# A planned attention and MLP kernel: w_in and w_out gated on block 1's values, the second buffer set's constant rows gated on w_out, and new planner constants

## The chip, the core and the metric

The kernel runs on one core of a Trainium2 chip. The time is the device time of one execution in microseconds (us). The core has five engines with their own instruction streams, which meet through semaphores: PE (TensorE, matrix products), ACT (ScalarE), DVE (VectorE), POOL (GpSimd) and SP (SyncE, which here only starts transfers). Transfers started by SP, ACT and POOL run on 16 DMA engines.

## The reference

Inputs are q, k, v of shape (4, 8, 768, 64), w_in (512, 2048) and w_out (2048, 512), all float32.

```python
ub = np.sum(np.maximum(q[:, :, :, None, :] * k_min[:, :, None, :, :],
                       q[:, :, :, None, :] * k_max[:, :, None, :, :]), axis=-1)
ub = np.where(causal, ub, -1000000000.0)
top_chunks = np.argsort(ub, axis=-1)[..., -top_k:]      # top 6 of 24 chunks of 32 keys
scores = scale * np.matmul(q, k.transpose(0, 1, 3, 2))
mask = sel & (pos[:, None] >= pos[None, :])
attn = softmax(np.where(mask, scores, -1000000000.0))   # written out in the reference
x = (attn @ v), heads put side by side                  # 3072 x 512
h = x @ w_in
g = np.maximum(h, 0.0) + np.log1p(np.exp(-np.abs(h)))
out = g @ w_out
```

So each query attends to the six chunks of keys with the highest upper bound, and the result goes through a two-layer MLP with a softplus.

## The kernel before, in words

**Blocks.** The queries are cut into 12 blocks of 256 rows: 4 batches of 3 blocks each. Block n belongs to batch n // 3. Each block has a preparation (`prep`), four attention units, one for each pair of heads (`attend`), and an MLP (`mlp_h`, `mlp_y`). The keys, values and chunk bounds of a batch live in one of two buffer sets, chosen by batch number modulo 2; block 3 is the first that uses the second set.

**Preparation.** k and q are transposed (blocks 0 to 2, the ramp, by PE at L515 and L572; later blocks by DMA at L534 and L582). DVE takes the maxima and minima of each chunk (L522, L538). ACT copies k into `ka` and `kb` (L519) and q into `qb` (L576); DVE makes the positive and negative parts of q (L591). PE computes the upper bounds (L611, L612), DVE masks them, finds the sixth largest and marks the chunks below it (L618 to L638). These marks are transposed (L659 or L674) and stand as extra rows in q; the matching extra rows of `ka` and `kb` hold a one-hot pattern of the chunks, so that the score matmul itself subtracts a large number for chunks not chosen.

**Attention.** For each head, L714 makes scores in PSUM, L723 takes the exponential on ACT, L729 cuts the diagonal on POOL, L740 multiplies by v, whose column of ones yields the sum; L749 and L761 normalize on DVE, and the result is transposed into x (L769, L774 in the ramp; by DMA at L777 later).

**MLP.** L797 multiplies x by w_in, L803 and L807 make the softplus on ACT as ln(1 + exp), L823 multiplies by w_out, L828 copies the result out of PSUM, L833 stores it.

**The planner.** The program is first built as a graph of tasks, each with an engine, a duration, a priority (a due time, lower first) and dependencies. `schedule` simulates the engines with these numbers: an engine that is free takes the ready task of lowest priority number for which buffers are free. The order found is then emitted, and each engine executes its part strictly in that order; what the hardware does later or earlier than planned doesn't change it. Before plan time `WARM` (30 us), whenever PE has nothing ready, the planner puts a filler in its stream, a matmul on a tile of zeros (L366).

Transfers have their own model: one started at plan time t enters its engine's queue `DMA_START` later; the queues share the DMA engines in proportion to a packet cost (`pkt`: 18 for block loads, 172 for a w_in half, 98 for a quarter of w_out); a transfer counts as landed `lat` after its last packet. At most 8 transfers of SP and ACT are under way.

**Loads.** Block loads of the ramp (`ramp_loads`, L398 and L401) come in two halves of 256 KB for each of q, k, v; they are issued in the order of `ORDER`. w_in comes in two transfers (i01, i23; L445), w_out in four (o0 to o3; L448), all issued by POOL, which converts them to bf16 on the way. Two kinds of holds tie these streams: `hold_pool` is a tiny POOL copy that reads a block's landed tile (L457), so that the weight loads behind it on POOL can't be issued earlier; `HOLDS` names the tile. `hold_sp` is a tiny SP transfer that reads a landed weight (L463), so that the loads behind it on SP can't be issued earlier. Before the change the first hold of POOL reads the second half of q of block 1 and stands ahead of w_in; SP's hold on the first w_in transfer stands ahead of k, q, v of block 2; POOL's second hold reads the second half of q of block 2 and stands ahead of w_out; SP's last hold (`LGATE`), on the third w_out transfer, stands ahead of the loads of block 3 and later blocks (L426).

**Due times.** `when_att` and `when_mlp` give each attention unit and MLP unit a due time. `MSTART` is where the MLP's due times start; `AOFF` and `AEND` say after how much MLP work the attention of blocks 3 to 11 begins and before how much of it that attention ends. `RLEAD` is how much earlier than its attention the preparation of blocks 0, 1, 2 is due, `POST` how much later the normalizing work of these blocks, `OPRIO` the priority of w_out's issue, `LEAD` how much earlier than the attention the loads of a later block are due.

**The second set's constants.** `background(1, ...)` (L349 to L355) clears `bd`, writes the column of ones of v, clears rows 0 to 31 of `kb` on DVE, and copies the one-hot rows into `ka` and `kb` by two POOL transfers.

Of the kernel before, what the change touches and what calls it, by code (L numbers as in the profile page):

```python
# [13 lines left out]
ACT = mybir.ActivationFunctionType  # L14
# [22 lines left out]
COLD = 4.2  # L37
TD = 1.9
TLAT = 1.4
RLEAD = (1, 1, -1)  # L40
POST = (0, 5, -2)
OPRIO = 15
LEAD = 18
BG = 40
DMA_START = 1.3
MSTART = 16
AOFF = 16
PADD = 0.0
PLEAD = 12
AEND = 26  # L50
ORDER = "k0 q0 k1 v0 q1 v1 i01 i23 k2 q2 v2 o0 o1 o2 o3".split()
HOLDS = [("q", 1, 1), ("q", 2, 1), ("q", 2, 1)]
SHIFT = (0, 0, 8)


# [21 lines left out]
class Graph:  # L77
# [7 lines left out]
    def add(self, eng, dur, fn, prio, r=(), w=(), dma=None, lat=None, name="", after=(), pkt=18, port=None, alt=None, at=0.0):  # L85
        t = Task()
        t.n, t.eng, t.dur, t.fn, t.prio, t.dma, t.name = len(self.tasks), eng, dur, fn, prio, dma, name
        t.lat = LAT[eng] if lat is None else lat
        t.pkt = pkt
        t.port = port if port is not None else eng == "POOL" and dma is None  # L90
        t.alts = {eng: (dur, fn, t.port)}
        if alt:
            t.alts[alt[0]] = (alt[1], alt[2], False)
        deps, bufs = set(after), []
        for key in list(r) + list(w):
            b = key[0] if isinstance(key, tuple) else key
            if isinstance(b, Buf) and b not in bufs:
                bufs.append(b)
        for key in r:
            if key in self.last:  # L100
                deps.add(self.last[key])
            self.readers.setdefault(key, []).append(t)
        for key in w:
            if key in self.last:
                deps.add(self.last[key])
            deps.update(x for x in self.readers.pop(key, ()) if x is not t)
            self.last[key] = t
        t.deps, t.users, t.bufs = deps, [], bufs
        for d in deps:
            d.users.append(t)  # L110
        for b in bufs:
            b.left += 1
        t.wait, t.ready, t.start, t.end, t.order = len(deps), at, None, None, None
        self.tasks.append(t)
        return t

    def schedule(self):
# [8 lines left out]
        def post(at, what, x):  # L126
            nonlocal seq
            seq += 1
            heapq.heappush(events, (at, seq, what, x))
# [59 lines left out]
        while True:  # L189
            nxt = events[0][0] if events else None  # L190
            live = [q for q in queues.values() if q]
            if live:
                total = sum(q[0][2] + (1 if len(live) > 1 else 0) for q in live)
                cand = moved + min(q[0][0] * total / q[0][2] for q in live)
                if nxt is None or cand < nxt:
                    nxt = cand
            if nxt is None:
                break
            now = max(now, nxt)
            flow(now)  # L200
            while events and events[0][0] <= now + 1e-9:
                _, _, what, x = heapq.heappop(events)
                if what == "ready":
                    for a in x.alts:
                        heapq.heappush(ready[a], (x.prio, x.n, x))
                elif what == "free":
                    free[x.pool].append(x.slot)
                    if x.kind:
                        used[x.pool, x.kind] -= 1
                elif what == "unlock":  # L210
                    x[0].held[x[1]] -= 1
                elif what == "landed":
                    x.end = now
                    done(x, now)
                elif what == "queue":
                    queues.setdefault(x.eng, []).append([x.dma, x, x.pkt])
            for e in LAT:
                if idle[e] > now + 1e-9 or not ready[e] and (e != "PE" or spare is None):
                    continue
                held, got = [], None  # L220
                while ready[e]:
                    item = heapq.heappop(ready[e])
                    if item[2].start is not None:
                        continue
                    if fits(item[2], e):
                        got = item[2]
                        break
                    held.append(item)
                for item in held:
                    heapq.heappush(ready[e], item)  # L230
                if e == "PE" and spare is not None and now >= WARM:
                    free["ps"].append(spare)
                    spare = None
                if got is None and e == "PE" and spare is not None and self.filler is not None \
                        and self.filler.deps and all(d.end is not None and d.end <= now for d in self.filler.deps):
                    self.fills.append((len(order), spare))
                    order.append(self.filler)
                    idle[e] = now + self.filler.dur * (2 if now < COLD else 1)
                    post(idle[e], "tick", None)
                if got is None:  # L240
                    continue
                t = got
                t.eng = e
                t.dur, t.fn, t.port = t.alts[e]
                if len(t.alts) > 1:
                    t.lat = LAT[e]
                for b in t.bufs:
                    if b.pool == "ps":
                        b.held[t.eng] = b.held.get(t.eng, 0) + 1
                    if b.slot is None:  # L250
                        b.slot = free[b.pool].pop(0)
                        if b.kind:
                            used[b.pool, b.kind] = used.get((b.pool, b.kind), 0) + 1
                t.start = now
                if t.port:
                    port[t.eng] = now + t.dur
                order.append(t)
                if e == "PE" and now < COLD:
                    t.dur *= 2
                idle[e] = now + t.dur  # L260
                post(idle[e], "tick", None)
                if t.dma is None:
                    t.end = now + t.dur + t.lat
                    done(t, t.end)
                else:
                    if e != "POOL":
                        flying.append(t)
                    post(now + DMA_START, "queue", t)
        assert len(order) == len(self.tasks) + len(self.fills), (len(order), len(self.tasks))
        return order  # L270

# [1 line left out]
def build(nc, tiles):  # L273
# [75 lines left out]
    def background(i, pr, after, blks):  # L349
        add("DVE", 0.2, lambda: DV.memset(T("bd", i), 0.0), pr, w=[("bd", i)], name="bd0", after=after)  # L350
        add("DVE", 0.1, lambda: DV.memset(T("v", i)[:, :, :, D:D + 1], 1.0), pr, w=[("v1", i)], name="v1", after=after)
        add("DVE", 1.35, lambda: DV.memset(T("kb", i)[0:32], 0.0), pr + 2, w=[("kb0", i)], name="kb0", after=after)
        for which in ("ka", "kb"):
            add("POOL", 0.6, lambda which=which: PO.dma_start(*oh(which, i, blks)), pr, r=["ohb"],
                w=[(which + "c", i, k_) for k_ in blks], name="oh" + which, after=after, dma=0.8, pkt=200, lat=0.7)  # L355
# [34 lines left out]
    def ramp_loads(nm, n, base, gate):  # L390
        for t in range(2):
            b_ = XF[nm, n, t] = Buf("xf")
            pr = base + 0.1 * t
            if n == 0 and nm != "v":
                for u, eng in ((0, "SP"), (1, "ACT")):
                    def ld(nm=nm, t=t, b_=b_, u=u, q_=AC if u else SP):
                        dst = T(b_).rearrange("s (t h d) -> s t h d", t=NT, d=D)
                        q_.dma_start(out=dst[:, u], in_=rows(nm, n, u)[:, t * 4:t * 4 + 4])  # L398
                    add(eng, 0.6, ld, pr, w=[(b_, u)], dma=0.585, lat=0.5, name=f"ld{nm}{n}{t}", after=gate)
            else:  # L400
                add("SP", 0.6, lambda nm=nm, t=t, b_=b_: SP.dma_start(  # L401
                    out=T(b_).rearrange("s (h d) -> s h d", d=D), in_=rows(nm, n, t)), pr,
                    w=[(b_, 0), (b_, 1)], dma=1.17, lat=0.5, name=f"ld{nm}{n}{t}", after=gate)


    def columns(nm, n, hh, p, t):
# [432 lines left out]
    for n in range(NRAMP):  # L839
        for p in range(NP):  # L840
            attend(n, p)
    background(1, BG, [landed["w_in", 3]], [0, 1, 2])
    for n in range(NB):
        m = n + NRAMP
        mlp_h(n)
# [114 lines left out]
```

## Time and profile before

| | |
|---|---|
| median of 7 runs | 261.6 us |
| lowest, highest | 260.17, 263.49 us |
| profiled execution, its own time | 260.04 us |
| span of its profile | 258.3 us |
| PE busy | 250.8 us (97%) |
| ACT busy | 202.9 us (79%) |
| DVE busy | 150.3 us (58%) |
| POOL busy | 84.5 us (33%) |
| HBM read, written | 27.26 MB, 6.29 MB |
| granted clock of PE | 0.999 of full |

The page of a profile gives busy times of the engines, the span in 40 slices (each digit the busy share in tenths), groups of instructions by line with their count and mean duration, and the transfers. The timeline lists instructions in order: start, length, engine, line, operation, written tile <- read tiles, form, count; an engine's idle time before an instruction and what ended it stand in brackets. PE's matmuls are pipelined: the length of one is longer than its distance to the next, so PE counts as busy where its starts are close. POOLq, SPq and so on stand for the issuing of a transfer, not for its running.

### The profile page before, as it was taken

The page shows a single profiled execution, that of the slowest core. Times are in us where ns is not written, and L with a number is a line of the kernel's source. Part 1 is how long each engine was busy: PE and PEld are TensorE (multiplying, and loading weights), DVE is VectorE, ACT ScalarE, POOL GpSimd, SP SyncE. Part 2 cuts the span into 40 slices and gives each one's busy share as a digit, 9 for nine tenths or more (in the row PEclk, how much of TensorE's full clock was granted, in tenths as well). Part 3 has the DMA queues.
Part 4 walks back from the last instruction along what each step waited for, and adds up shares of the span by engine and source line. Part 5 has one row for each costly group of instructions (what it writes and reads, how often), then busy time and mean ns, then how long its engine had stood idle before and what let it go on. Part 6 is the DMA issues. An engine that isn't in the chain of part 4 may idle for free.

```text
span 258.3 us, 6762 instructions
## 1 busy us (share of the span) xinstructions
PE 250.8 (97%) x2563; PEld 191.5 (74%) x2594; DVE 150.3 (58%) x549; ACT 202.9 (79%) x369; POOL 84.5 (33%) x179
## 2 busy tenths in 40 slices
PE   8999999999999999999999999999999999999994
PEld 6989996687685885788677678777677777776763
DVE  7797565347796699546998586665964211211101
ACT  5795999999296995899679779968689799666470
POOL 5180470255235470354805425235022111100000
PEclk9999999999999999999999999999999999999999
DMA  7989999999996996998679899649511220230202
GB/s 174 255 144 213 251 183 188 219 239 228 185 260 129 235 219 137 271 193 189 145 181 241 170 224 197 154 123 206 121 44 41 43 82 3 23 102 0 82 2 82
DMA packets 119993, 39.90 MB, mean 154 GB/s; under 512 B 113528, under 2 KB 115832, under 8 KB 119960
## 3 DMA queue, kind: packets, MB, share of 16 engines
q1 hardware_dynamic: 114456, 34.09, 60.5%
q0 software_dynamic: 3392, 4.85, 10.5%
q10 hardware_dynamic: 2112, 0.52, 0.9%
q8 instruction: 20, 0.33, 0.5%
q14 instruction: 13, 0.11, 0.1%
HBM read 27.26 MB, written 6.29 MB: 130 GB/s over the span
## 4 chain that ended last, share of the span: by engine, by line
PE 80%; DMA 10%; DVE 3%; SPq 2%; POOL 2%; issue 2%; ACT 0%; DVEq 0%
PE ps L823 28%; PE ps L797 28%; PE ps L714 12%; PE ps L740 7%; DMA w_out_sb<-in_moe_w_out_dram 5%; DMA w_in_sb<-in_moe_w_in_dram 3%; PE ps L366 3%; DMA w<-in_q_dram 2%; SPq L401 2%; POOL w_out_sb L448 1%; PE ps L515 1%; PE ps L612 1%; POOL pt L729 1%; DVE kx L538 1%; PE ps L611 1%
## 5 line engine op out<-in xcount | busy, mean ns | idle before, releaser
L797 PE MATMUL ps<-x,w_in_sb 128*128 128x256 bf16 x768 | 101.6, 272 | 0.2
L723 ACT ACTIVATE pt<-ps 128x512 bf16<-128x512 f32 (+1 forms) x192 | 94.2, 609 | 8.6 <-PE ps L714 8.3
L823 PE MATMUL ps<-w_out_sb,g 128*128 128x512 bf16 (+1 forms) x369 | 92.0, 370 | 1.5 <-DMA w_out_sb<-in_moe_w_out_dram 0.2
L797 PEld LDWEIGHTS <-w_in_sb 128*128 128x128 bf16 x768 | 72.4, 98 | 15.1
L729 POOL TENSOR_SCALAR_AFFINE_SELECT pt<-pt 128x256 bf16<-128x256 bf16 x96 | 40.2, 425 | 123.4 <-ACT pt L723 123.3
L803 ACT ACTIVATE e<-ps 128x512 f32<-128x512 f32 x96 | 59.8, 646 | 26.5 <-PE ps L797 26.2
L823 PEld LDWEIGHTS <-g 128*128 128x128 bf16 x400 | 36.7, 98 | 25.7 <-ACT g L807 0.6
L807 ACT ACTIVATE g<-e 128x1024 bf16<-128x1024 f32 x48 | 52.6, 1095 | 1.0
L828 DVE COPY yo<-ps 128x512 f32<-128x512 f32 (+1 forms) x25 | 16.7, 669 | 41.1 <-PE ps L823 40.9
L749 DVE RECIPROCAL st<-ps 128x4 f32<-128x4 f32 x48 | 8.5, 179 | 43.5 <-PE ps L740 38.3
L714 PE MATMUL ps<-qab,kb 128*128 128x256 bf16 x192 | 30.6, 259 | 0.1
L740 PEld LDWEIGHTS <-pt 128*128 128x128 bf16 x672 | 26.4, 97 | 4.2
L714 PE MATMUL ps<-qab,ka 96*128 96x256 bf16 x192 | 29.1, 259 | 0.1
L740 PE MATMUL ps<-v,pt 128*128 128x65 bf16 x672 | 28.1, 193 | 0.1
L436 POOL CAST w<-w 128x512 bf16<-128x512 f32 x36 | 22.5, 637 | 2.2 <-DMA w<-in_k_dram 1.8
L538 DVE TENSOR_REDUCE kx<-w 128x32 bf16<-128x1024 bf16 x18 | 21.2, 1208 | 0.1
L714 PEld LDWEIGHTS <-ka 96*128 96x128 bf16 x192 | 17.5, 98 | 5.1 <-issue 0.2
L714 PEld LDWEIGHTS <-kb 128*128 128x128 bf16 x192 | 16.6, 97 | 5.3
L366 PE MATMUL ps<-zero 128*128 128x256 bf16 x118 | 17.2, 290 | 1.1 <-DVE zero L336 1.1
L761 DVE TENSOR_TENSOR w<-ps,st 128x256 bf16<-128x256 f32 x36 | 15.1, 422 | 1.2
L627 DVE MAX8 ub<-ub 128x8 f32<-128x24 f32 (+2 forms) x160 | 14.5, 163 | 0.3
L366 PEld LDWEIGHTS <-zero 128*128 128x128 bf16 x118 | 11.5, 104 | 2.9 <-DVE zero L336 1.1
(64 smaller groups left out, 179.5 us busy)
## 6 DMA issues: line engine op xcount, KB each, us to landing
w<-in_v_dram SPq DMA_DIRECT2D x24, 256.0 KB, 4.4
out_dram<-yo SPq DMA_DIRECT2D x23, 256.0 KB, 2.2
w<-in_k_dram SPq DMA_DIRECT2D x22, 256.0 KB, 3.8
w<-in_q_dram SPq DMA_DIRECT2D x22, 256.0 KB, 4.2
w_in_sb<-in_moe_w_in_dram POOLq DMA_DIRECT2D x2, 1024.0 KB, 10.5
w_out_sb<-in_moe_w_out_dram POOLq DMA_DIRECT2D x4, 512.0 KB, 8.6
w<-in_k_dram SPq DMA_DIRECT2D x2, 128.0 KB, 3.0
w<-in_k_dram ACTq DMA_DIRECT2D x2, 128.0 KB, 3.6
```

The costliest lines, as they stand in the source:

```text
L366: PE.matmul(T(Fill)[:, 0:256], T("zero")[:, 0:128], T("zero"), start=True, stop=True)
L436: PO.tensor_copy(T(b_)[:, :, t], T(xf).rearrange("s (p c) -> s p c", p=NP))
L538: DV.tensor_reduce(T(kx)[:, m].rearrange("d p (t c) -> d p t c", t=NT), T(kt).rearrange("d (p t) (c s) -> d p t c s", t=NT, s=CH), axis=AX ...
L714: PE.matmul(T(sp)[:, z * QB:z * QB + QB - q0], kk[r0:r1, p, (j + z) * 128:(j + z + 1) * 128], qq[r0:r1, p, q0:QB], start=True, stop=True)
L723: AC.activation(T(pt)[:, j:j + 2].rearrange("k j c -> k (j c)")[:, 0:w], T(sp)[:, 0:w], ACT.Exp, scale=SCALE)
L729: PO.affine_select(out=diag, in_=diag, compare_op=ALU.is_ge, fill=0.0, base=0, channel_multiplier=-1, pattern=[[0, 2], [1, 128]])
L740: PE.matmul(o[:, u, h], T(pts[h])[:, j, c0:c0 + 128], T("v", i)[:, j, 2 * p + h, :], start=(j == 0), stop=(j == t0 + u))
L797: PE.matmul(o, T("w_in")[:, dt, ft * 128:(ft + 1) * 128], T(x)[:, dt], start=(dt == 0), stop=(dt == KDM - 1))
L803: AC.activation(T(e)[:, f2 * 2:f2 * 2 + 2].rearrange("f a s -> f (a s)"), T(hp), ACT.Exp)
L807: AC.activation(T(gb)[:, f4 * 4:(f4 + 1) * 4], T(e), ACT.Ln, bias=1.0)
L823: PE.matmul(T(y)[:, 0:w], T(gb)[:, f, u * 128:(u + 1) * 128], T("w_out")[:, f, cs], start=(f == 0), stop=(f == KFF - 1))
L828: add("DVE", 0.06 + 0.54 / parts, lambda y=y, yo=yo, w=w: DV.tensor_copy(T(yo)[:, 0:w], T(y)[:, 0:w]), pr, r=[y], w=[yo], name=f"yo{n}")
```

## The change

Ten planner constants get other values; `DMA_START` becomes a table, with 2.5 us for POOL's transfers instead of 1.3; the planned landing latency of the ramp's block loads goes from 0.5 to 0.7 us. `ORDER` puts k, q, v of block 2 ahead of the weights: with that, SP's hold between the first w_in transfer and block 2's loads no longer exists, POOL's second hold ahead of w_out no longer exists, and the one hold left, ahead of all six weight transfers, reads the first half of v of block 1. `LGATE` still reads the third w_out transfer. The second set's constants wait in the plan for the second w_out transfer instead of the second w_in transfer.

```diff
-RLEAD = (1, 1, -1)
-POST = (0, 5, -2)
-OPRIO = 15
-LEAD = 18
+RLEAD = (3, 6, 3)
+POST = (2, 0, 0)
+OPRIO = 20
+LEAD = 14
 BG = 40
-DMA_START = 1.3
-MSTART = 16
-AOFF = 16
+DMA_START = {"SP": 1.3, "ACT": 1.3, "POOL": 2.5}
+MSTART = 18
+AOFF = 8
 PADD = 0.0
 PLEAD = 12
-AEND = 26
-ORDER = "k0 q0 k1 v0 q1 v1 i01 i23 k2 q2 v2 o0 o1 o2 o3".split()
-HOLDS = [("q", 1, 1), ("q", 2, 1), ("q", 2, 1)]
+AEND = 20
+ORDER = "k0 q0 k1 v0 q1 v1 k2 q2 v2 i01 i23 o0 o1 o2 o3".split()
+HOLDS = [("v", 1, 0), ("k", 2, 1), ("k", 2, 1)]
...
-                    post(now + DMA_START, "queue", t)
+                    post(now + DMA_START[e], "queue", t)
...
-                    add(eng, 0.6, ld, pr, w=[(b_, u)], dma=0.585, lat=0.5, name=f"ld{nm}{n}{t}", after=gate)
+                    add(eng, 0.6, ld, pr, w=[(b_, u)], dma=0.585, lat=0.7, name=f"ld{nm}{n}{t}", after=gate)
...
-                    w=[(b_, 0), (b_, 1)], dma=1.17, lat=0.5, name=f"ld{nm}{n}{t}", after=gate)
+                    w=[(b_, 0), (b_, 1)], dma=1.17, lat=0.7, name=f"ld{nm}{n}{t}", after=gate)
...
-    background(1, BG, [landed["w_in", 3]], [0, 1, 2])
+    background(1, BG, [landed["w_out", 1]], [0, 1, 2])
```

## The prediction, made before the changed kernel was run

> **What bounds the kernel now.** I read the page's busy times first, then the slices, then the timeline of the first 50 us, the spacing of matmuls over the whole trace, and ACT's busy time by stretch.
>
> ```profile
> PE 250.8 (97%) x2563; PEld 191.5 (74%) x2594; DVE 150.3 (58%) x549; ACT 202.9 (79%) x369; POOL 84.5 (33%) x179
> ...
> PE   8999999999999999999999999999999999999994
> ...
> DMA  7989999999996996998679899649511220230202
> ...
> L366 PE MATMUL ps<-zero 128*128 128x256 bf16 x118 | 17.2, 290 | 1.1 <-DVE zero L336 1.1
> ```
>
> PE looks full everywhere, but line 366 is the planner's filler: 118 matmuls on zeros, all before 23.4 us, 14.4 us by their start-to-start spacing. Useful matmuls had used only 7.9 us when the first MLP matmul (L797) started at 24.34. After that the spacing shows almost no holes up to the last matmul start at 254.7: records missing from the trace leave about 31 apparent gaps of 0.22 us, and the larger ones are 0.72 us at 92.2, 0.48 at 67.1, 0.32 at 49.3. True waiting after 24.34 is about 1.5 us, and 3.6 us follow the last start. So the time is set by how much useful PE work is done by about 25 us, and by not opening holes later: 258.3 us = 14.4 filler + about 2 of early waiting + 1.5 + 3.6 + about 237 of work and its ordinary spacing.
>
> The start of the MLP hangs on the first w_in half:
>
> ```profile
> 15.52 0.18 POOL L457 CAST scratch<-w 1x1 bf16<-1x1 f32 x1
> 15.65 1.53 POOL L445 DMA_DIRECT2D w_in_sb<-in_moe_w_in_dram  x2
> 16.65 0.64 PE L572 MATMUL ps<-identf,w 128*128 128x128 f32 x4
> ...
> 23.51 0.55 PE L714 MATMUL ps<-qab,ka 96*128 96x256 bf16 x4
> ...
> 23.71 0.29 DVE L774 COPY x<-ps 128x256 bf16<-128x256 bf16 x1 [0.22 <-PE ps L769]
> ...
> 23.85 0.75 SPq L463 DMA_DIRECT2D scratch<-w_in_sb  x1
> ...
> 24.34 0.60 PE L797 MATMUL ps<-x,w_in_sb 128*128 128x256 bf16 x4
> ...
> 34.99 3.02 POOL L448 DMA_DIRECT2D w_out_sb<-in_moe_w_out_dram  x4
> ...
> 40.50 1.90 PE L823 MATMUL ps<-w_out_sb,g 128*128 128x512 bf16 x7
> ```
>
> The reader sees hold, w_in issue, w_in landed (SP's hold passes at 23.85), first MLP matmul; block 1's first scores (L714) and the end of block 0's last copy into x fall at the same moment. w_out follows only at 34.99 and its first use waits at 40.50. In the packets, the block loads stream without a break from 2.0 to 15.4 us (256 KB each 1.05 us), then nothing moves until 17.3; w_in takes 17.3 to 28.0, block 2's loads 28 to 35.5, another hole of 1.2 us, w_out 36.4 to 48.2.
>
> The second bound is ACT, by stretch:
>
> ```profile
> 20.00:24.34 4.34, 1.89 (x4) 1.00 1.12 212
> 24.34:35.00 10.66, 10.66 (x23) 1.00 1.18 250
> 35.00:40.00 5.00, 4.93 (x9) 1.00 0.84 139
> ```
>
> Second column: length of the stretch, then ACT's busy time. It idles 2.45 us just before the MLP starts and then has none to spare for 15 us.
>
> **The change, part by part.** Filler and order are fixed by the planner, so I work its constants by hand for positions only; durations are the trace's. Plan time plus 0.8 is trace time here: w_in's first landing is planned at 22.85, so 23.65, and SP passed at 23.85.
>
> 1. Gate of w_in. In the plan block loads take 1.17 each; the second part of q1 ends at 14.87, the first of v1 at 16.04, and landing is 0.5, now 0.7, later. The hold moves from 15.37 to 16.74; with start 2.5 for 1.3 and the k2 loads beside it (rate 172/192, so 4.9 becomes 5.47), w_in's first landing is planned at 25.57, 26.4 in trace time. The first MLP matmul goes from 24.34 to 26.4 to 27.0: **2.0 to 2.7 us later**, with filler or other work ahead of it. The data itself hardly moves: the old hold did not wait for q1 at all but for the four selects before it on POOL (14.00 to 15.57). One or two more selects (0.4 each, their exps done by 17) may now stand before it: issue 15.7 to 17.3, landing 8.2 later, 24 to 25.5, plus sharing with k2. So mostly the plan, not the data, is late.
>
> 2. What fills these 2 us. Block 1's prep gets priority 6 ahead of its time instead of 1, ahead of block 0's post (2 later). From qT (16.65) to its first scores (23.5) the chain took 6.8 us. In it, block 0's work stands on DVE: two reciprocals and two normalizations after 19 us (0.18 + 0.41 each, 1.2 in all) and one pair with an x copy before 18.1 (0.9); on ACT an exp and an x copy stand between the two qb copies (0.9, beside the DVE work). So scores start 1.2 to 2.1 earlier, 21.4 to 22.3. Four exps take 1.9 us (0.48 each): 8 to 10 of 16 by 26.4, with three more scores in flight 11 to 13 at 0.22 or 0.16, some 2.3; one or two pairs of value products (14 x 0.029 = 0.41 each); and the transposes of k2, landed by 18 because its loads now follow v1 directly (8 x 0.109 = 0.87). Useful PE work by 26.4 was 9.85 before; now 6.92 (all before the first scores) + 0.2 + 2.3 + 0.4 to 0.8 + 0.87 = 10.7 to 11.1, or 10.2 with late scores. Ahead by 0.4 to 1.2.
>
> 3. Keeping it. From 24.34 to 35 ACT was full, so PE's lead survives only as far as ACT too is ahead. It is, by what it uses of the 2.45 idle: 1.2 to 2.1, less k2's copies taken early. Steps 1 to 3: between 0 and 1.9, I take **-0.9**, the middle.
>
> 4. w_out. Its issue moves from 34.99 to about 20 (POOL is 0.76 per issue and free from 19.6 to 25). Queue 0 needs 10.7 + 11.5 = 22.2 us of packets; from about 18 that ends at 40.2, or 44 if all of block 2's 6 loads not yet moved (6.3 less 2.6 moved in today's hole) go first. Before it was 48.2. The first output matmul can leave 40.5 for about 35; the waits at 40.5 and 49.3 and their neighbours go, about 0.5. **-0.4**; not more, because PE had other matmuls to do while it waited.
>
> Who yields is not in the trace for this pair. Nearest rows: k2, issued at 25.04, got not one packet until 27.7 while w_in ran, which gives the block loads no share; the one-hot transfer at 30.25 to 31.0 left q2 a share of about 0.37 of the packets' time. I take a tenth (17 ns packets against 173); the ends put w_in's first landing later by 0 to 3.0 us.
>
> The Trainium skill ("DMA: Bandwidth & Descriptors", Queues, rings and completion order) says an engine round-robins between queue rows a packet of several descriptors at a time; by it w_in would lose a share from its first packet, where the row at 25 to 27.7 shows block loads getting none. With equal turns this would be the tenth I take, 0.6 us on the first half; by the row alone 0.
>
> 5. Block 2. k2 comes 10 us sooner, q2 and v2 trickle behind the weights: q2 is planned at 41.4 (its transposes were at 37.7), v2 at 47 to 48.5. If they get no share at all they land at 42 to 45, about as planned. From q2's transposes to the first scores took 37.7 to 47.05; ACT alone made qb wait until 41.15. With priority 4 us earlier I count 5.5 us: 47 again. **0**, within 1.5 either way. LGATE, the hold ahead of block 3's loads, waits for w_out at about 41 instead of 46.2, but block 3 queues behind v2 on SP: free.
>
> 6. Zero and one-hot rows of the second set: 1.34 + 0.22 + 0.10 on DVE and two POOL issues of 0.57 leave 28.5 to 31.5 for after 38. DVE was busy 3.2 of 5 from 40 to 45, POOL 0: cost 0; without that cover up to 1.7 in block 2's chain. First needed by block 3, loaded after 47.
>
> 7. AOFF, AEND, MSTART, LEAD spread the attention of blocks 3 to 11 from 8 instead of 16 us after the MLP's start to 20 instead of 26 before its end. ACT, idle half of 60 to 70 us, gets exps sooner. The last value products were at 222.9, x of the last block is transposed at 223.9, its MLP needs 13.9: 6 us later still fits. At stake are the 1.2 us at 67 and 92: at best gone, at worst another pair like it. **-0.3**.
>
> Sum -1.6: the profiled execution's 260.04 becomes 258.4. It lies 1.6 below the median of 261.6, so in medians **260.0**.
>
> **Rivals.** A measurement of this kernel tells a change of 0.5%, 1.3 us, from none.
>
> A, forecast: 258.7 to 261.3 around 260.0; 0.45 (0.29 faster, 0.16 within).
>
> B, larger gain: ACT turns all 2.45 idle us into exps, and the waits of 1.5 go: -4.0, 257.6. For it: ACT is the second bound from 24 to 40. Against it: DVE was busy 4.32 of 5 from 20 to 25, so the scores can't start much sooner. 0.17.
>
> C, the change does little: the lead is given back while ACT is full and PE fills its queue; 261.6. For it: the old gate did not wait on its data, and w_in's real landing barely moves. 0.11.
>
> D, slower: the MLP starts 2.0 to 2.7 us later behind filler and block 1's scores do not come earlier, since DVE stays the limit of its prep. That decides if the first scores start after about 23; each later us of the start is then a us of the end. +2.0 to 2.7: 263.6 to 264.3. For it: nearly all PE time after 24.34 is work, so nothing later can absorb it. Sharing w_in's transfer three to one, as in step 4's upper end, comes to the same place. 0.27 (0.25 slower).
>
> Faster 0.47, within 0.5% 0.27, slower 0.26. Range 257.2 to 264.4: B's and D's ends.
>
> **What would show it.** Right: filler ends near 26, first MLP matmul at 26 to 27 with useful PE work above 10.2 us by 26.4; first scores of block 1 before 22.4; packets without the hole at 15.4; w_out landed by 44; first output matmul near 35; ACT busy above 3 of 4.34 in 20 to 24.34. Wrong: PE holes above 0.5 us on w_in or q2; first scores after 23; new holes after 60.

## The result and the profile after

The changed kernel takes 262.75 us (median of 13 runs, 261.98 to 263.39), the kernel before 261.29 (32 runs, 260.17 to 263.49): ratio 1.0057, 95% interval 1.0037 to 1.0076. It is slower, where the forecast was faster; the time lies within the range given. The profiled executions are 262.68 (span 261.0) and 260.04, 2.64 apart against 1.46 of the medians, because the profiled one of before lies at its low end.

The page of the kernel after (busy times, two rows of slices, the fillers' group):

```profile
PE 252.3 (97%) x2572; PEld 192.7 (74%) x2604; DVE 149.7 (57%) x553; ACT 201.6 (77%) x365; POOL 83.2 (32%) x178
...
PE   8999899999899999999999999999999999999994
...
DMA  7999999899894897999684599847930410111202
...
L366 PE MATMUL ps<-zero 128*128 128x256 bf16 x128 | 19.3, 288 | 1.1 <-DVE zero L336 1.1
```

PE looks as full as before, but ten more of its matmuls are fillers: 128, the last at 27.55, 16.0 us by their spacing. What moved is in the timeline of the first 40 us:

```profile
17.03 0.18 POOL L457 CAST scratch<-w 1x1 bf16<-1x1 f32 x1
17.15 0.60 POOL L685 CAST v<-w 128x512 bf16<-128x512 f32 x1
17.71 1.57 POOL L445 DMA_DIRECT2D w_in_sb<-in_moe_w_in_dram  x2
18.59 13.09 SPq L401 DMA_DIRECT2D w<-in_v_dram  x2
...
21.23 1.31 DVE L627 MAX8 ub<-ub 128x8 f32<-128x16 f32 x16
21.37 2.99 POOL L448 DMA_DIRECT2D w_out_sb<-in_moe_w_out_dram  x4
24.31 0.38 PE L714 MATMUL ps<-qab,ka 96*128 96x256 bf16 x2
27.33 0.49 PE L366 MATMUL ps<-zero 128*128 128x256 bf16 x3
27.66 0.59 PE L740 MATMUL ps<-v,pt 128*128 128x65 bf16 x14
28.94 0.61 PE L797 MATMUL ps<-x,w_in_sb 128*128 128x256 bf16 x4 [0.69 <-DMA w_in_sb<-in_moe_w_in_dram]
38.08 1.02 PE L823 MATMUL ps<-w_out_sb,g 128*128 128x512 bf16 x3 [0.30 <-DMA w_out_sb<-in_moe_w_out_dram]
```

Against before: w_in is issued 2.06 us later (17.71 for 15.65), block 1's first scores start 0.8 later (24.31 for 23.51), the first MLP matmul 4.6 later (28.94 for 24.34), the first output matmul 2.4 earlier. The page's last part, DMA issues with the size of each and the us to landing, before and then after:

```profile
w_in_sb<-in_moe_w_in_dram POOLq DMA_DIRECT2D x2, 1024.0 KB, 10.5
w_out_sb<-in_moe_w_out_dram POOLq DMA_DIRECT2D x4, 512.0 KB, 8.6
```

```profile
w_in_sb<-in_moe_w_in_dram POOLq DMA_DIRECT2D x2, 1024.0 KB, 13.7
w_out_sb<-in_moe_w_out_dram POOLq DMA_DIRECT2D x4, 512.0 KB, 20.6
```

w_out's 20.6 is mostly queueing, since it is issued at 21.37, behind w_in; w_in's 13.7 is not. Its first half took 8.19 us from issue to landing and now 11.19. The packets show why: before, 103 packets of 2 KB go per us; after, 87, with 85 packets of block 2's loads (256 B) beside them, one for one. Of the 16 engines' landings of this half, thirteen come by 26.55 (8.84 after issue), the rest at 27.01, 27.94 and 28.90. In each later part of the weights the last three or four engines lag again, the last of them 2.1 to 2.4 us behind the twelfth.

Useful PE work (no fillers) up to a time, in us, each recorded matmul counted at the usual spacing of its form, with each run's profiled execution and its ratio to the kernel before (the runs are told below):

```
            24.34   26.4     30     35     60    240  profiled   ratio
before       7.90   9.85  13.43  18.39  41.55 213.01   260.04
b_ramp       7.41   8.83  12.35  17.30  39.62 211.52   261.89   0.9989
d_q0         6.97   8.87  12.36  16.77  39.38 210.84   261.93   0.9992
after        7.96   8.93  10.97  15.81  39.24 210.21   262.68   1.0057
x_less       7.85   8.94  11.68  16.65  40.80 211.51   261.31   1.0011
x_data       7.85   8.82  11.46  16.37  41.16 217.32   261.96   1.0014
b_order      7.09   8.01   8.34  10.97  35.05 200.91   272.30   1.0342
```

The table counts recorded matmuls. Of L823's 368 large ones (0.215 us each) some 30 are missing from each trace but x_data's, so x_data's entry at 240 stands up to 6.9 us too high and its entry at 60 somewhat; between the other rows, 0.4 us at 240 can be records alone. The profiled execution of before is 1.25 below its median, so its row flatters it. b_ramp and d_q0 tie with it by the ratio and were profiled near their medians: after is 1.0 to 1.5 behind these two at 35 and 0.6 to 1.3 at 240. In after, the spacing shows two holes of PE on weights that are late, 0.86 us at 28.06 (w_in) and 0.46 at 37.51 (w_out): 1.32 together, where the medians differ by 1.46. (The brackets of the timeline show 0.69 and 0.30 of them, since the length it gives a matmul is longer than its spacing.)

### The profile page after: what moved, and what is told of

Its sections match the earlier page's. It is cut to its first block, busy times and chain, and to the rows that moved or that the text cites. A ratio compares the mean times of both kernels' runs of the same rounds, so it can differ in the third digit from the quotient of the medians.

```text
span 261.0 us, 6780 instructions
## 1 busy us (share of the span) xinstructions
PE 252.3 (97%) x2572; PEld 192.7 (74%) x2604; DVE 149.7 (57%) x553; ACT 201.6 (77%) x365; POOL 83.2 (32%) x178
## 4 chain that ended last, share of the span: by engine, by line
PE 79%; DMA 9%; DVE 5%; ACT 2%; issue 2%; POOL 1%; ACTq 0%; DVEq 0%
PE ps L823 29%; PE ps L797 27%; PE ps L714 12%; DMA w_out_sb<-in_moe_w_out_dram 8%; PE ps L740 6%; PE ps L366 4%; DVE kx L538 2%; ACT pt L723 2%; DMA qab<-w 1%; DVE qpn L591 1%; PE ps L572 1%; PE ps L612 1%; POOL w_out_sb L448 1%; PE ps L611 1%; DVE osb L761 0%
## 5 line engine op out<-in xcount | busy, mean ns | idle before, releaser
L797 PE MATMUL ps<-x,w_in_sb 128*128 128x256 bf16 x768 | 101.5, 272 | 0.7 <-DMA w_in_sb<-in_moe_w_in_dram 0.7
L823 PE MATMUL ps<-w_out_sb,g 128*128 128x512 bf16 (+1 forms) x368 | 91.8, 370 | 1.9 <-DMA w_out_sb<-in_moe_w_out_dram 0.3
L797 PEld LDWEIGHTS <-w_in_sb 128*128 128x128 bf16 x768 | 72.4, 98 | 15.9 <-DMA w_in_sb<-in_moe_w_in_dram 0.8
L803 ACT ACTIVATE e<-ps 128x512 f32<-128x512 f32 x96 | 59.0, 640 | 29.5 <-PE ps L797 28.9
L729 POOL TENSOR_SCALAR_AFFINE_SELECT pt<-pt 128x256 bf16<-128x256 bf16 x96 | 39.5, 417 | 130.4 <-ACT pt L723 130.4
L823 PEld LDWEIGHTS <-g 128*128 128x128 bf16 x400 | 36.9, 98 | 26.3 <-issue 0.7
L740 PE MATMUL ps<-v,pt 128*128 128x65 bf16 x672 | 28.4, 193 | 0.1
L714 PE MATMUL ps<-qab,ka 96*128 96x256 bf16 x192 | 28.0, 259 | 0.4 <-DVE qab L664 0.3
L436 POOL CAST w<-w 128x512 bf16<-128x512 f32 x36 | 21.9, 631 | 2.8 <-DMA w<-in_q_dram 2.8
L538 DVE TENSOR_REDUCE kx<-w 128x32 bf16<-128x1024 bf16 x18 | 21.4, 1210 | 0.1
L366 PE MATMUL ps<-zero 128*128 128x256 bf16 x128 | 19.3, 288 | 1.1 <-DVE zero L336 1.1
L366 PEld LDWEIGHTS <-zero 128*128 128x128 bf16 x128 | 12.3, 103 | 2.8 <-DVE zero L336 1.1
## 6 DMA issues: line engine op xcount, KB each, us to landing
w_in_sb<-in_moe_w_in_dram POOLq DMA_DIRECT2D x2, 1024.0 KB, 13.7
w_out_sb<-in_moe_w_out_dram POOLq DMA_DIRECT2D x4, 512.0 KB, 20.6
```

Of the source, the lines that this page charges most:

```text
L366: PE.matmul(T(Fill)[:, 0:256], T("zero")[:, 0:128], T("zero"), start=True, stop=True)
L436: PO.tensor_copy(T(b_)[:, :, t], T(xf).rearrange("s (p c) -> s p c", p=NP))
L538: DV.tensor_reduce(T(kx)[:, m].rearrange("d p (t c) -> d p t c", t=NT), T(kt).rearrange("d (p t) (c s) -> d p t c s", t=NT, s=CH), axis=AX ...
L714: PE.matmul(T(sp)[:, z * QB:z * QB + QB - q0], kk[r0:r1, p, (j + z) * 128:(j + z + 1) * 128], qq[r0:r1, p, q0:QB], start=True, stop=True)
L729: PO.affine_select(out=diag, in_=diag, compare_op=ALU.is_ge, fill=0.0, base=0, channel_multiplier=-1, pattern=[[0, 2], [1, 128]])
L740: PE.matmul(o[:, u, h], T(pts[h])[:, j, c0:c0 + 128], T("v", i)[:, j, 2 * p + h, :], start=(j == 0), stop=(j == t0 + u))
```

## The experiments

Names: `b_` runs are the kernel before with a part of the change, `a_` runs the kernel after without a part, `x_` runs the kernel after with a new edit. Each ratio is to the kernel before on the same chip.

**The parts.** Order means `ORDER`, `HOLDS` and the gate of the second set; model means `DMA_START` and the latencies; ramp means `RLEAD` and `POST`; steady means `MSTART`, `AOFF`, `AEND`, `LEAD`, `OPRIO`.

```diff
# a_plan: after, transfer model as before
-DMA_START = {"SP": 1.3, "ACT": 1.3, "POOL": 2.5}
+DMA_START = {"SP": 1.3, "ACT": 1.3, "POOL": 1.3}
# and lat=0.7 -> 0.5 at L399 and L403
```

> The changed kernel with the planner's transfer model put back: start of POOL's transfers 1.3 instead of 2.5, landing latency of the ramp's loads 0.5 instead of 0.7. The plan then has w_in 1.4 us sooner and fewer fillers, the transfers themselves are the same. T: PE waits at the first MLP matmul for w_in's true landing near 28.5: 262.2 to 262.8. P: 261.3. S: 262.7.

271.47 us, 1.0355 [1.0306, 1.0404]. Here PE waits 2.38 us for w_in at 25.79, and 2.2 us at 73 (its timeline):

```profile
72.81 2.34 DVE L538 TENSOR_REDUCE kx<-w 128x32 bf16<-128x1024 bf16 x2
75.18 0.42 DVE L677 COPY qab<-w 32x1024 bf16<-32x1024 bf16 x1
75.65 0.66 PE L714 MATMUL ps<-qab,ka 96*128 96x256 bf16 x6 [2.04 <-DVE qab L677]
```

A plan that expects w_in too early puts MLP matmuls where PE can only wait; at 73 DVE does L538 ahead of the L677 that PE waits for. After each of the two holes the granted clock is halved for 3.4 us (last section), which is part of the 9 us.

```diff
# b_order: before with the new order alone; a_order: after with the old order
-HOLDS = [("q", 1, 1), ("q", 2, 1), ("q", 2, 1)]
+HOLDS = [("v", 1, 0), ("k", 2, 1), ("k", 2, 1)]
# and ORDER, and the gate landed["w_in", 3] <-> landed["w_out", 1]
```

> The kernel before with only the new ORDER, HOLDS and gate of the second set's constants; the old transfer model and due times. T: w_in lands at 27 to 29, PE waits for it at the first MLP matmul: 1.5 to 4 us above before. S and R: within 0.5 us of before.

> The changed kernel with the old ORDER, HOLDS and gate of the second set's constants; all other constants and the new transfer model stay. T (the loss is w_in's late arrival, by later issue and by sharing with block 2's loads): w_in lands near 24 again, first MLP matmul at 24.5 to 26, no worse than before: 260.5 to 262.0 where before has 261.3 to 262.1. Rival S (the due times after 30 us): stays 1 to 2 us above before. Rival R (the ramp's new leads delay block 1's scores): stays above before by about 1, first scores of block 1 after 24.

b_order 271.54, 1.0342 [1.0296, 1.0387]; a_order 266.04, 1.0156 [1.0121, 1.0191]. b_order has the same wait as a_plan, and then a window at half the clock (the number before the last two):

```profile
29.45 1.03 PE L797 MATMUL ps<-x,w_in_sb 128*128 128x256 bf16 x4 [3.00 <-DMA w_in_sb<-in_moe_w_in_dram]
```

```profile
28.40:35.20 6.80, 5.75 (x39) 4.40 (x40) 0.60 (x2) 2.78 (x6) 1.22 (x3) 0.50 1.15 201
```

a_order fits none of the three theories: w_in lands at 25.20 and the first MLP matmul follows at 25.24, but PE waits for DVE (holes of 1.46 us at 38.53 and 0.63 at 40.10), has another hole at 88.49 (1.44), and the clock is halved from 42.2 to 45.6.

```diff
# b_model: before with the new model. b_om: with the new order and model.
```

> The kernel before with only the new transfer model (POOL's transfers start 2.5 after issue, ramp loads land 0.2 later). The plan puts the first MLP matmul 1.2 to 1.4 us later behind fillers, while w_in lands at 23.9 as before. If each us of a later start is a us of the end: 1 to 1.6 us above before. If block 1's scores and DVE fill the time: within 0.5 us.

> The kernel before with the new ORDER, HOLDS and gate, and the new transfer model; old leads and due times. The order alone cost 3.4%, the changed kernel without its model 3.6%. If the model is what pays that back (a plan that knows how late w_in is puts other work and fillers ahead instead of a wait): 0.3 to 1% above before, no hole of over 1 us at the first MLP matmul. If the due times pay it back: 3% or more above.

b_model 262.18, 1.0020 [0.9998, 1.0043]; b_om 266.1, 1.0161 [1.0120, 1.0201]. So the model costs nothing that can be told, and takes the order's cost from 3.4% to 1.6%; part of that is the clock, which was halved twice in b_order's profile and never in b_om's. b_om keeps a hole of 2.0 us at 72 like a_plan's.

```diff
# b_ramp: before with the new RLEAD, POST. a_ramp: after with the old ones.
```

> The kernel before with only the new RLEAD and POST. R: block 1's scores start no earlier than 23.5, or later, and the kernel is 1 us or more above before. T: w_in lands at 23.9 as before, the first MLP matmul moves by at most 0.7 either way, and the time is within 1 us of before. The recorded prediction's step 2 expected first scores at 21.4 to 22.3.

> The changed kernel with the old RLEAD and POST. T2: as the changed kernel, 0.4 to 0.8% above before, since these two alone did nothing to the kernel before. T3: 1% or more above. The recorded prediction's step 2 (they bring block 1's scores forward): later first scores and about 1 us slower than the changed kernel.

b_ramp 261.86, 0.9989 [0.9962, 1.0016]; a_ramp 262.38, 1.0024 [0.9995, 1.0054]. With the leads alone, block 1's first scores start at 24.11, not earlier than 23.51. In the new order and model the leads do bring them forward: without them they start at 26.20 in a_ramp and at 25.91 in b_om, with them at 24.31 in after. b_ramp, a_ramp, b_om:

```profile
24.11 0.55 PE L714 MATMUL ps<-qab,ka 96*128 96x256 bf16 x4
```

```profile
26.20 0.76 PE L714 MATMUL ps<-qab,ka 96*128 96x256 bf16 x6
```

```profile
25.91 0.76 PE L714 MATMUL ps<-qab,ka 96*128 96x256 bf16 x6
```

So the first half of what a_ramp was expected to show came true (later scores), and the second did not: it is no slower than after, whose scores come 1.9 us sooner.

```diff
# b_steady: before with the new MSTART, AOFF, AEND, LEAD, OPRIO. a_steady: after with the old ones.
```

> The kernel before with only the new MSTART, AOFF, AEND, LEAD and OPRIO. S: 1 us or more above before, with new holes on PE after 50 us. T: the first 25 us as before, the time within 0.8 us of before.

> The changed kernel with the old MSTART, AOFF, AEND, LEAD and OPRIO. These alone cost the kernel before 0.7%. If they cost the same here (T2: the parts add up), 260.9 to 261.7, 0.2% below to 0.1% above before. If they were chosen for the new order (T3: the parts only work together), 264 or more.

b_steady 263.83, 1.0067 [1.0038, 1.0096]; a_steady 262.62, 1.0026 [0.9995, 1.0057]. a_steady lies between its two theories; its profiled execution, 264.09, the longest of its twelve, has holes where after has them, 0.68 us at 28.90 and 0.79 at 41.65. In b_steady PE comes to w_out too early and waits, and the clock is halved from 41.9 to 45.3:

```profile
41.02 1.07 PE L823 MATMUL ps<-w_out_sb,g 128*128 128x512 bf16 x3 [2.24 <-DMA w_out_sb<-in_moe_w_out_dram]
```

The parts do not add: alone they give +3.4%, +0.2%, -0.1% and +0.7%, together +0.57%.

**The shared transfer.** One theory: block 2's loads beside w_in delay it and PE starts late. Rival: the order of the plan alone costs the time.

```diff
 # x_hold: after; ldq21, ldv20, ldv21 issued behind a hold on w_in's first half
...
+if t.name == "ldw_in" and first is None:
+    first = t
+    nc.sync.dma_start(out=fixed["scratch2"][0:1, 0:2], in_=fixed["w_in"][0:1, 0, 0:2])
+    for u in late:
+        u.fn()
```

> The changed kernel, with the planner's order kept on every engine but SP: the last three of block 2's loads (second half of q, both halves of v) are issued behind a hold on the first w_in transfer. Theory T (the loss is the late first MLP matmul, at 28.95 instead of 24.34; w_in lands at 28.90 because its packets share with block 2's loads, 3.0 us of it): w_in lands near 26, but PE's ordered stream reaches the first MLP matmul only at 28.06, so at most 0.9 us is won: 261.9 to 262.4 where the changed kernel has 262.75. Rival S (the loss comes from the new due times after 30 us): no change, 262.7. Rival Q (q and v of block 2 are the late ones): slower, over 263, since they come later still.

262.8, 1.0028 [0.9998, 1.0057]; w_in lands 9.62 us after its issue, but q2 is now late and PE waits 1.74 us at 39.87. A shift of the trouble, and inconclusive.

```diff
 # c_k2: before, with k2 alone ahead of w_in
-ORDER = "k0 q0 k1 v0 q1 v1 i01 i23 k2 q2 v2 o0 o1 o2 o3".split()
+ORDER = "k0 q0 k1 v0 q1 v1 k2 i01 i23 q2 v2 o0 o1 o2 o3".split()
```

> The kernel before with only k of block 2 moved ahead of the first w_in transfer; q and v of block 2 stay behind SP's hold on it, all gates and constants as before. k2's 2.1 us of packets fit into the 1.8 us in which the DMA engines had nothing to move, so T (sharing with w_in is what delays it) expects w_in at 23.8 to 24.6, w_out 1 to 2 us earlier, and a time from 1.5 us below before to equal. If any block load ahead of w_in delays it by several us: w_in after 26 and 1.5 us or more above before.

264.09, 1.0090 [1.0055, 1.0126]. Two 256 KB loads beside w_in suffice to delay it: 84.5 packets of w_in and 83 of k2 per us from 20 to 22, landing 10.36 us after issue.

```profile
26.51 0.61 PE L797 MATMUL ps<-x,w_in_sb 128*128 128x256 bf16 x4 [1.40 <-DMA w_in_sb<-in_moe_w_in_dram]
```

Its 0.9% is not the price of that wait alone: PE also waits at 86 for DVE, and the clock is halved from 90.6 to 94.0:

```profile
89.12 0.54 PE L714 MATMUL ps<-qab,ka 96*128 96x256 bf16 x4 [2.41 <-DVE qab L677]
```

```diff
 # x_less: after; q2's second half and v2 load one head of eight (the rest is set to 0)
+hs = slice(0, 1) if n == 2 and (nm, t) in (("q", 1), ("v", 0), ("v", 1)) else slice(0, H)
...
 # x_less_nofill: the same, without the last 16 fillers
```

> The changed kernel in its own order, but the second half of q and both halves of v of block 2 bring only one head of eight each (the other heads are zeros written by POOL early on, so the output is not the reference's): sharing with w_in nearly ends, and q2 isn't late as in the run with the hold. T (the data come late): w_in lands at 26 to 27 instead of 28.9, PE reaches the first MLP matmul in its order at 28.0, first w_out at 35 to 36: 0.9 to 1.5 us below the changed kernel, so within 0.3 us of before. Plan only (P): no more than 0.3 us below the changed kernel, 0.4 to 0.6% above before.

> The same, also without the 16 fillers ahead of the first MLP matmul. If late data and late order cover each other (T), the first MLP matmul comes at 26.5 to 27.3 and the time goes 1 us or more below the run with the fillers, 0.3% or more below before. If block 1's chain of scores sets when PE gets there, fillers or not, nothing is won: within 0.5 us of the run with the fillers.

x_less 262.0, 1.0011 [0.9987, 1.0035], at the same order of instructions; x_less_nofill 263.3, 1.0064 [1.0033, 1.0095]. x_less (its lines count one higher):

```profile
28.16 0.60 PE L798 MATMUL ps<-x,w_in_sb 128*128 128x256 bf16 x4
36.82 1.03 PE L824 MATMUL ps<-w_out_sb,g 128*128 128x512 bf16 x3
```

Here w_in lands 10.17 us after its issue and w_out's first part at 35.50 instead of 38.04; the first MLP matmul comes 0.8 earlier, the first output matmul 1.3. Both holes of after, 0.86 and 0.46, are gone, and the ratio falls by 0.46%, 1.2 us. PE, ACT and DVE execute the same instructions in the same order in both traces, so they can be laid side by side: from the first on, the same L797 matmuls come 0.8 us earlier in x_less, by 40 us 1.26, at 70 us 2.0, and from 135 us to the end 1.37 (the spans differ by 1.36). So nearly all of the gain is made at these two holes. That is the account of the loss.

```diff
 # x_data: all six loads of block 2 one head of eight; hold and w_in issues ahead of the fourth select
+move = [t for t in order if t.name in ("hold", "ldw_in") and t.eng == "POOL"]
+order = [t for t in order if t not in move]
+at = [i for i, t in enumerate(order) if t.name == "cm0"][3]
+order[at:at] = move
 # x_data_short: also the last 16 fillers 16 columns wide instead of 256
```

> The changed kernel with PE's, ACT's and DVE's order kept, but the data as early as they can be: all six loads of block 2 bring one head of eight (the rest zeros from POOL, so the output is not the reference's), and POOL issues w_in ahead of its fourth select and the v copy. w_in should land at 24, w_out's first part near 31. PE gets to the first MLP matmul in its order at 27.5 to 28.0, as in the changed kernel but for the wait. T (late data): 0.5 us above to 0.7 below the run with fewer loads, at or below before. P (the planned order, with fillers for a w_in at 26.4): the 2 us that the first MLP matmul stays late are not won back, 0.1 to 0.5% above before still.

> The same, with the last 16 fillers cut from 256 to 16 columns: the number of instructions and their place stay, so nothing shifts in the code as it did when they were left out, but they take about 0.03 instead of 0.109 us each, 1.3 us less in all. P: the first MLP matmul at 26.5 to 27, 0.3% to 0.5% below the former. If block 1's scores (from 24.3) set when PE gets there: the same first MLP matmul within 0.4 us and no gain.

x_data 261.92, 1.0014 [0.9993, 1.0034]; x_data_short 261.85, 1.0017 [0.9996, 1.0037]. x_data, then x_data_short:

```profile
16.27 1.54 POOL L446 DMA_DIRECT2D w_in_sb<-in_moe_w_in_dram  x2
...
27.97 0.59 PE L741 MATMUL ps<-v,pt 128*128 128x65 bf16 x14
28.39 0.60 PE L798 MATMUL ps<-x,w_in_sb 128*128 128x256 bf16 x4
```

```profile
25.56 0.27 PE L939 MATMUL ps<-zero 128*128 128x16 bf16 x5
26.42 0.54 PE L715 MATMUL ps<-qab,kb 128*128 128x256 bf16 x4 [0.59 <-ACT pt L724]
28.22 0.63 PE L741 MATMUL ps<-v,pt 128*128 128x65 bf16 x14
```

Both holes are gone here too. In x_data w_in is there at 24.61, and yet PE reaches L798 only at 28.39. Not the fillers hold it: shortened, their place is taken by waits on the exps of block 1 (L724 frees the score tiles), and the value products of 27.97 move to 28.22. The MLP stands behind block 1's scores and value products in PE's order, and these start at 24.62 in x_data.

**The fillers.** 

```diff
 # x_nofill: after without the last 16 fillers; x_both: x_nofill and x_hold
+if t is graph.filler:
+    fills += 1
+    if fills > 112:
+        continue
...
```

> The changed kernel without its last 16 fillers, those that stand in PE's stream from about 24.3 us to the first MLP matmul; all other work keeps its place. T: PE reaches the first MLP matmul earlier and waits there for w_in, landing at 28.9: 262.5 to 262.8, no gain alone. If the fillers themselves were the loss (rival P, the plan alone): about 1.7 us less, 261.0. S: 262.7.

> Both of the former: block 2's last three loads behind the first w_in transfer, and the last 16 fillers left out. T: the late data and the late order cover each other, so only both together win: the first MLP matmul near 26.5 to 27, 260.6 to 261.4. P: 261.0, as without fillers alone. S: 262.7. Q: over 263.

x_nofill 263.93, 1.0068 [1.0034, 1.0102]; x_both 263.91, 1.0060 [1.0032, 1.0087]: nothing gained. Both, and x_less_nofill, have a hole of 1.7 to 2.1 us at 87 to 91, which x_data_short with its narrow fillers has not; in x_nofill PE waits for x of block 3, which comes by a transfer:

```profile
90.98 0.27 PE L797 MATMUL ps<-x,w_in_sb 128*128 128x256 bf16 x1 [1.52 <-DMA x<-w]
```

Why it follows from the fillers was not tried. x_nofill also issues w_in 1.14 us later than after (18.85), so it is no clean test. x_less_nofill reaches the first MLP matmul at 28.2, no sooner than x_less: there too the fillers were not what held it.

**The hold.** 

```diff
 # d_q0: before
-HOLDS = [("q", 1, 1), ("q", 2, 1), ("q", 2, 1)]
+HOLDS = [("q", 1, 0), ("q", 2, 1), ("q", 2, 1)]
```

> The kernel before with its first hold on the first instead of the second half of block 1's q: in POOL's order w_in's issue then stands ahead of one of the four selects that kept it until 15.65. w_in lands 0.4 to 1.2 us sooner, and w_out too. T: 0 to 1 us below before, since x of block 0 is ready only at 24.0 and the gain is in what follows. If orders made anew by the planner differ by more than that by chance: up to 4 us above.

261.39, 0.9992 [0.9973, 1.0012]. No run beats the kernel before by more than its interval.

## Why the prediction was wrong, step by step

The loss is two waits of PE on weights, 0.86 for w_in and 0.46 for w_out's first part. At the same order of instructions x_less is without them, and 1.0057 falls to 1.0011; x_data, with w_in 3.3 us earlier still, gains nothing more (1.0014), since PE's order reaches the MLP at 28.4 in any case. Both intervals take in 1: what is left of the loss cannot be told from nothing. Both kernels of this test move fewer bytes, so block 3's loads come earlier in them too (41.4 for 45.6 in x_less); but 1.26 of the 1.36 us are won by 40 us, before these are issued.

The rival, the order of the plan, explains instead why there is no gain. The planner (`build` and `schedule` of each kernel) runs without the chip, and its own plan could have been read: it ends at 255.76 us for before and at 256.85 for after, so it holds no gain, and it has block 1's first scores at 22.41 in before, 22.75 in after and in b_ramp, and 23.84 in b_om and a_ramp, an order that the traces keep. It is no forecast of the time: for b_model, which measured as before, it ends at 259.21.

- **Step 1, gate.** Issue at 17.71 lies past its 15.7 to 17.3: the v copy (0.60 at 17.15) stands between hold and issue and was not counted. In the plan w_in's first half lands at 26.16, not at the 25.57 worked by hand. First MLP matmul 28.94 instead of 26.4 to 27.0.
- **Step 2, what fills the gap. Failed.** Scores were put at 21.4 to 22.3; they started at 24.31. The step took before's 23.5 as its base and put what the rest of the change does to it at nothing: with the new order and model but the old leads the scores start 2.7 us later (26.20, a_ramp), and the leads win back 1.9. Block 0's work did leave DVE's way, but the two halves of block 1 now go through each stage together. Before, DVE did the first half's 8 MAX8 at 20.25 and the second's at 22.05:

```profile
20.25 0.68 DVE L627 MAX8 ub<-ub 128x8 f32<-128x16 f32 x8
...
22.05 0.68 DVE L627 MAX8 ub<-ub 128x8 f32<-128x16 f32 x8
```

After, all 16 come in one run from 21.23 (the timeline above), and the first half's marks wait for the second's maxima. In b_ramp, which has the leads without the order, the marks of both halves (L635, L638) run in one stretch, 22.00 to 22.92, and the scores start at 24.11, so the leads alone gain nothing on the old plan. Which part of the new order and model pushes the scores back was not tried apart; b_model (24.96) and b_order (24.91) each do. Useful work by 26.4 was 8.93, not 10.2 to 11.1: fillers took the gap.
- **Step 3, keeping it.** Nothing to keep. ACT's windows (length, ACT's busy time) show it:

```profile
20.00:24.34 4.34, 2.71 (x7) 1.00 1.02 178
24.34:35.00 10.66, 9.68 (x22) 1.00 1.15 203
35.00:40.00 5.00, 4.77 (x7) 1.00 1.21 195
```

0.8 more than before in the first stretch, 1.0 less in the second. That ACT then waits for PE's scores and MLP is argued from the order, not shown.
- **Step 4, w_out and sharing. Mis-sized.** A tenth, 0.6 us, was taken, with 3.0 as the upper end; measured 3.0. For thirteen engines 0.65 holds, but the landing is the sixteenth's, 2.35 later. The row at 25 to 27.7, where k2 got no packet, does not carry over: loads that are under way when w_in begins take equal turns with it (c_k2). Why k2 got none there stays open. The Trainium skill ("DMA: Bandwidth & Descriptors", Queues, rings and completion order) has an engine take turns between its queue rows, a whole packet at a time; 87 against 85 recorded packets per us agrees with equal turns. Instead of -0.4, PE waited 0.86 and 0.46 us. First output matmul 38.08, not 35.
- **Step 5, block 2.** Put at 47, within 1.5 either way; its first scores came at 48.77, just outside.
- **Steps 6, 7.** No cost of the constants shows. The due times gain nothing: holes of 0.47 and 0.46 us stay at 65.7 and 67.9, and alone they cost 0.67% (b_steady), some of it by the halved clock.
- **Rivals.** D's condition, scores after 23 and a late MLP, came true, and its 2.0 to 2.7 us fit the profiled executions (2.64); the medians give 1.46, below its range. Its price, a us of the end for each us that the MLP starts later, is not what was measured: the MLP starts 4.6 us later in after, and 1.67 later in b_model (26.01), which is at 1.0020. Its upper end of step 4 came true as well. It had 0.27 and the forecast 0.45, since two gains in a row (earlier scores, little sharing) had each been taken at the better reading.
- **Slips without weight.** The range's ends, 257.2 and 264.4, are not quite those of B and D (257.6 and 264.3), and a block-load packet alone takes 18 ns, not 17.

**Open:** why three engines lag; why a_steady, with both holes in its profile, reads 1.0026 and not more (its interval overlaps with after's); and what makes the executions of before differ by 3 us.

## What to carry to other kernels

A large transfer lands with its last engine: price what is put beside it from its landing, not from the mean rate, and give a load its own time if the next stage waits for it. A planner's constants work only together: the same order cost 3.4%, 1.6% or 0.6% with other due times and a better model of the transfer. Where the order comes from a planner that can be run, read its plan before working parts of it by hand. A lead is to be priced on the plan it will stand in: here it won 1.9 us of scores there and lost 0.6 on the old plan.

## What the runs showed of the hardware

The stream of 256 B packets took a turn for each 2 KB packet, at 31 ns of its own time instead of 18. SP's issue of v2's two loads lasted 13.09 us (18.59 in the timeline above; 1.03 for the first, 12.01 for the second) while block loads and weights ran together, and SP issued nothing else in that time.

The granted clock fell to a half in several runs, after holes of PE. In a_plan it was halved from 29.7 to 33.1, after the hole at 25.79, and from 77.5 to 80.9, after the one at 73; the windows around the second give length, then the busy time of PE, PEld, DVE, ACT and POOL, the clock, DMA share and GB/s:

```profile
72.00:74.00 2.00, 1.25 (x32) 1.02 (x28) 1.83 (x5) 0.68 (x2) 0.41 (x1) 1.00 1.12 217
74.00:76.00 2.00, 0.35 (x5) 0.33 (x5) 1.94 (x4) 0.00 (x0) 0.00 (x0) 1.00 0.70 159
76.00:78.00 2.00, 1.33 (x19) 0.92 (x18) 1.93 (x7) 1.99 (x5) 0.88 (x2) 0.87 1.24 278
78.00:80.00 2.00, 2.00 (x31) 1.78 (x30) 2.00 (x20) 1.17 (x4) 2.00 (x6) 0.50 1.05 304
```

In the profiles, one hole of 2.06 to 3.16 us by the spacing was followed by such a stretch each time (a_plan and b_order twice, b_steady, c_k2, x_less_nofill), of 3.4 us, or 6.8 in b_order; single holes of 1.68 to 2.01 us were not (x_nofill, x_hold, x_both, b_ramp, b_om), but a_order's 1.46 and 0.63 close together were. It is not the same in each execution: the mean clock was 0.991 to 0.994 in three of b_om's six and 0.994 in three of x_less_nofill's nine, and 0.998 or more in the rest. A stretch of 3.4 us at half the clock costs up to 1.7 us of PE's work (an estimate: half its length), so a hole can cost more than its length; neither before nor after has one in the middle of its profile. The Trainium skill ("TensorE: Matmul & The Clock Gate", What's actually happening) names an idle window of about 3.4 us; no hole here was as long, so by these traces shorter ones can be enough.
